# Output stores moved from SyncE's list to ScalarE's, in an attention and spatial-gate kernel

## The chip, the cores and the metric

The kernel runs on one core of a Trainium2 chip. A core has five engines with a list of instructions each: TensorE (PE, with its weight loads shown as PEld), VectorE (DVE), ScalarE (ACT), GpSimd (POOL) and SyncE (SP). An engine takes its list in order; engines wait for one another by semaphores. Transfers between HBM and the core's SBUF go over 16 DMA engines; an instruction on an engine's list issues them, and they run on their own afterwards. The metric is the device time of one execution in microseconds (us).

## The reference

For each of 8 batches and 8 heads, 576 tokens with 64 values each are first pooled into 32 memory slots, then attend to the slots; the result of all heads (512 values a token) goes through a gated feed-forward block whose gate mixes the tokens.

```python
a = softmax(phi, axis=slots)                      # 8 x 8 x 576 x 32
k_m, v_m = a^T k, a^T v                           # 32 x 64 per head
attn = softmax(q k_m^T / 8) v_m
x = attn, heads side by side                      # 8 x 576 x 512
h = relu(x @ w_in); u, v = halves of h            # 1024 -> 512 + 512
v_n = (v - mean) / sqrt(var + 1e-6)
v_s = w_spatial @ v_n + b_spatial                 # mixes the 576 tokens
out = (u * v_s) @ w_out                           # 8 x 576 x 512, float32
```

## The kernel before

The work goes batch by batch. A batch's 576 tokens are four tiles of 128 and a remainder of 64. Large products are made of three products of rounded parts (`fp32r`, a high and a low part of each factor), which is why most of PE's lines come in threes.

The stages are Python generators, each cut into steps by `yield`: `memory_weights` (loads phi, its exponentials), `memories` (loads k and v; product `kvm` over the tokens, line 342, and the scaled copies `kmn`, line 369, on ACT), `queries` (loads q in four pieces, transposes), `scores`, `products` (slots times `w_in`), `gate` (v's half: product `pv`, lines 621 and 630/631, its copies `vr`, lines 626 and 640 to 642, the normalization, and `vh`, line 663), `units` (u's half: product `pu`, line 687, read by ACT into `u`, line 696), `spatial` (the mixing, `ps`, line 725, and the gated product) and `project` (product `po`, line 765, and the output).

`project` is the stage at the change. It makes twelve matmuls into one PSUM bank `po` for a tile of 128 tokens; ACT copies the bank to an SBUF tile `o` (line 771); in the step after that, SP issues the store (line 774). The remainders of two batches share one tile: in every odd batch a fifth `po` is made, and it is stored by two issues, one for each batch (lines 776 and 777). So a batch has four or five copies, and the kernel has 36 copies and 40 stores.

What sets the order is written out by hand: three strings, `START`, `PLAN` (one pass for each of the batches 1 to 6) and `LAST`, list the steps; a letter names the stage (`O` for `project`), a digit the tile, a mark how many batches ahead. Each engine's list follows the order of the steps. While one batch is projected, the next one's gate and memory weights are on the way. A step of a store stands some steps behind the one of its copy.

Buffers: `o` has two, from the pool `two`, so a copy waits until the store two copies ago has landed. PSUM has four single banks (pool `ps1`: `po`, `pv`, `kvm` and others in turn) and two double ones (pool `ps2`: `pu`, `ps`), so PE's third `pu` needs the buffer that ACT empties by reading the first into `u`. A transfer counts on one of eight semaphores in turn, and an issue waits until the transfer before it on the same semaphore has landed, if that is not known from earlier waits.

All loads and stores are on SP's list. In a batch of the loop it holds: two stores, the phi load, two q loads, a store, the k load, the remaining stores, the v load, two more q loads.

Of the kernel before, what the change touches and what calls it, by code (L numbers as in the profile page):

```python
# [55 lines left out]
def memory_attention_spatial_gate(  # L56
# [29 lines left out]
    nc = tc.nc  # L86
    B, H, S, D = q.shape
# [3 lines left out]
    P = 128  # L91
    NI = 4
    SM = NI * P
    SR = S - SM
# [13 lines left out]
    def bank(name):  # L108
        return ps1.tile([P, 512], F32, tag="b1", name=name)
# [642 lines left out]
    def project(b, st):  # L752

        if st == NI and b % 2 == 0:
            return
        po = bank(f"po_{b}_{st}")
        n = 0
        for dt in range(NJ):
            if st < NI:
                h_, l_ = (x[:, dt, st * P : (st + 1) * P] for x in state["g", b])  # L760
            else:
                h_, l_ = (x[:, dt, :] for x in state["rem"])
            woh, wol = (x[:, dt % 2] for x in state["wo", dt // 2])
            for a, w in ((h_, woh), (h_, wol), (l_, woh)):
                nc.tensor.matmul(po, a, w, start=(n == 0), stop=(n == 11))  # L765
                n += 1
            if dt == 1:
                yield
        yield
        o = two.tile([P, DM], F32, name="o")  # L770
        nc.scalar.copy(o, po)  # L771
        yield
        if st < NI:
            nc.sync.dma_start(out[b, st * P : (st + 1) * P], o)
        else:
            nc.sync.dma_start(out[b - 1, SM:S], o[0:SR])
            nc.sync.dma_start(out[b, SM:S], o[SR:P])
        yield


    def warm_up(b, _):
# [13 lines left out]
    BATCH = {  # L795
        "P": memory_weights, "K": memories, "Q": queries, "S": scores, "M": products,
        "V": gate, "U": units, "G": spatial, "O": project,
    }
    threads, done = {}, {}
# [66 lines left out]
```

## Time and profile before

| what | us |
|---|---|
| median of 3 runs | 416.6 (416.01 to 416.63) |
| the profiled execution | 417.52 |
| its span, first to last instruction | 415.7 |
| PE busy | 401.5 (97%) |
| PE weight loads busy | 339.3 (82%) |
| DVE busy | 283.8 (68%) |
| ACT busy | 230.0 (55%) |
| POOL busy | 46.5 (11%) |

The granted TensorE clock is 0.8 of full speed in the second to fourth of forty slices of the span and 0.9 or more in the others. The 16 DMA engines are busy 42% of the span, in bursts. A row of the timeline gives an instruction's start from the start of the span and its duration; what stands in brackets is how long its engine had been idle and which instruction ended that. Issues of DMAs are work of an engine's sequencer (`SPq`) and are not counted as busy time.

### The profile page before, as it was taken

How to read it: one execution, taken by the hardware profiler on the slowest of the kernel's cores; microseconds unless marked ns; L12 is line 12 of the kernel's file. 1: busy time of each engine (PE TensorE's matmuls, PEld its weight loads, DVE VectorE, ACT ScalarE, POOL GpSimd, SP SyncE). 2: the span in 40 equal slices, each digit the busy share in tenths (PEclk: the TensorE clock that was granted, in tenths of full speed). 3: DMA queues.
4: the chain of work that ended last, by engine and by line, in shares of the span. 5: the costliest groups of instructions: out<-in, count | busy, mean ns of one | idle time of the engine just before them, and what ended most of it. 6: DMA issues, size and time to landing. Idle time of an engine off the chain costs nothing.

```text
span 415.7 us, 9467 instructions
## 1 busy us (share of the span) xinstructions
PE 401.5 (97%) x3965; PEld 339.3 (82%) x3965; DVE 283.8 (68%) x540; ACT 230.0 (55%) x425; POOL 46.5 (11%) x131
## 2 busy tenths in 40 slices
PE   6789999999999999999999999999999999999996
PEld 3544788989798888978798888988798788989984
DVE  1477999986988468947888468947887368924430
ACT  2468889546644476337644476347734476348321
POOL 1000321003200210003200210003200210013000
PEclk9888999999999999999999999999999999999999
DMA  8899595035810891039500990049401510020003
GB/s 297 320 383 279 116 342 142 2 107 111 236 50 31 176 301 24 0 105 276 123 2 17 247 258 7 0 117 290 97 2 37 101 50 0 2 76 27 0 30 97
DMA packets 85790, 50.70 MB, mean 122 GB/s; under 512 B 66226, under 2 KB 70322, under 8 KB 85748
## 3 DMA queue, kind: packets, MB, share of 16 engines
q1 hardware_dynamic: 85748, 50.10, 42.0%
q8 instruction: 31, 0.51, 0.5%
q14 instruction: 11, 0.09, 0.1%
HBM read 40.65 MB, written 9.44 MB: 120 GB/s over the span
## 4 chain that ended last, share of the span: by engine, by line
PE 87%; DMA 4%; DVE 4%; ACT 3%; issue 1%; SPq 0%; ACTq 0%
PE ps L725 29%; PE po L765 22%; PE pu L687 12%; PE pv L621 10%; PE kvm L342 3%; PE mp L589 3%; PE sc L523 2%; DMA w_rem<-in_moe_w_spatial_dram 2%; DMA q_all<-in_q_dram 1%; PE idle L785 1%; PE pv L630 1%; PE pv L631 1%; DMA out_dram<-o 1%; PE tq L410 1%; PE wt L255 1%
## 5 line engine op out<-in xcount | busy, mean ns | idle before, releaser
L725 PE MATMUL ps<-wth,vh 128*128 128x288 f32 x256 | 57.1, 304 | 0.0
L725 PE MATMUL ps<-wth,vl 128*128 128x288 f32 x256 | 54.8, 296 | 0.0
L725 PE MATMUL ps<-wtl,vh 128*128 128x288 f32 x256 | 54.5, 294 | 0.0
L765 PE MATMUL po<-woh,gl 128*128 128x512 f32 x128 | 50.4, 394 | 0.0
L765 PE MATMUL po<-woh,gh 128*128 128x512 f32 x128 | 50.4, 394 | 0.0
L645 DVE BATCH_NORM_STATS2 st<-vr 128x6 f32<-128x512 f32 (+1 forms) x40 | 27.0, 675 | 34.1 <-ACT vr L626 33.3
L765 PE MATMUL po<-wol,gh 128*128 128x512 f32 x128 | 50.2, 392 | 0.0
L725 PEld LDWEIGHTS ps<-wth,vh 128*128 128x128 f32 x256 | 41.2, 190 | 8.7 <-ACT vh L663 5.0
L650 POOL TENSOR_SCALAR rs<-mv 128x1 f32<-128x1 f32 (+1 forms) x40 | 8.8, 221 | 330.4 <-DVE grl L749 153.4
L747 ACT CAST gh<-g 128x512 fp32r<-128x512 f32 x32 | 19.8, 621 | 46.4 <-DVE g L736 45.2
L771 ACT COPY o<-po 128x512 f32<-128x512 f32 x36 | 21.0, 584 | 37.3 <-PE po L765 20.0
L725 PEld LDWEIGHTS ps<-wth,vl 128*128 128x128 f32 x256 | 41.1, 188 | 0.0
L725 PEld LDWEIGHTS ps<-wtl,vh 128*128 128x128 f32 x256 | 41.1, 188 | 0.0
L736 DVE TENSOR_TENSOR g<-u,ps 128x576 f32<-128x576 f32 x32 | 23.4, 751 | 17.1 <-PE ps L725 17.1
L665 DVE TENSOR_TENSOR vl<-vr,vh 128x512 fp32r<-128x512 f32 x32 | 21.6, 681 | 18.0 <-ACT vh L663 17.8
L660 ACT ACTIVATE vr<-vr,sh,rs 128x512 f32<-128x512 f32 (+1 forms) x40 | 32.1, 816 | 3.0 <-POOL sh L655 3.0
L626 ACT ACTIVATE vr<-pv 128x512 f32<-128x512 f32 x32 | 19.2, 600 | 19.4 <-PE pv L621 13.1
L687 PE MATMUL pu<-ah,mh 128*128 128x288 f32 x128 | 28.7, 306 | 0.0
L765 PEld LDWEIGHTS po<-wol,gh 128*128 128x128 f32 x128 | 24.1, 188 | 5.2
L765 PEld LDWEIGHTS po<-woh,gl 128*128 128x128 f32 x128 | 24.1, 188 | 5.2
L765 PEld LDWEIGHTS po<-woh,gh 128*128 128x128 f32 x128 | 24.0, 188 | 5.2
L687 PE MATMUL pu<-al,mh 128*128 128x288 f32 x128 | 27.4, 296 | 0.0
(141 smaller groups left out, 861.3 us busy)
## 6 DMA issues: line engine op xcount, KB each, us to landing
kv_sb<-in_k_dram SPq DMA_DIRECT2D x8, 1152.0 KB, 7.0
kv_sb<-in_v_dram SPq DMA_DIRECT2D x8, 1152.0 KB, 7.7
out_dram<-o SPq DMA_DIRECT2D x32, 256.0 KB, 2.3
q_sb<-in_q_dram SPq DMA_DIRECT2D x28, 288.0 KB, 5.6
phi_sb<-in_phi_dram SPq DMA_DIRECT2D x8, 576.0 KB, 5.0
raw<-in_moe_w_in_dram SPq DMA_DIRECT2D x8, 512.0 KB, 10.3
raw<-in_moe_w_out_dram SPq DMA_DIRECT2D x4, 512.0 KB, 6.0
q_all<-in_q_dram SPq DMA_DIRECT2D x1, 1152.0 KB, 5.4
```

The source lines that it names most:

```text
L342: nc.tensor.matmul(kvm[r][32 * j : 32 * j + 32], phi_sb[halves[r], j, i, :], kv_sb[halves[r], j, :, i * D : (i + 1) * D], start=(i == 0), ...
L621: nc.tensor.matmul(pv, x[:, r, cs], m[:, r, DM:DFF], start=(n == 0), stop=(n == 5))
L626: nc.scalar.activation(vr, pv, AF.Relu)
L645: nc.vector.bn_stats(st6, vr)
L660: nc.scalar.activation(vr, vr, AF.Identity, bias=sh, scale=rs)
L665: nc.vector.tensor_tensor(vl[:, st, :], vr, vh[:, st, :].bitcast(F32), op=ALU.subtract)
L687: nc.tensor.matmul(pu[:, hf, 0:HALF], m[:, r, cs], a[:, r, hf * HALF : (hf + 1) * HALF], start=(n == 0), stop=(n == 5),)
L725: nc.tensor.matmul(ps[:, hf, 0:HALF], a, w[:, hf * HALF : (hf + 1) * HALF], start=(n == 0), stop=(n == len(ops) - 1),)
L736: nc.vector.tensor_tensor(g.rearrange("p (a s) -> p a s", a=2), u[:, dt, :].rearrange("p (a s) -> p a s", a=2), ps[:, :, 0:HALF], op=ALU.mult,
L747: nc.scalar.copy(hi, x)
L765: nc.tensor.matmul(po, a, w, start=(n == 0), stop=(n == 11))
L771: nc.scalar.copy(o, po)
```

## The change

The three calls that issue the stores are made on ScalarE's queue.

```diff
         nc.scalar.copy(o, po)
         yield
         if st < NI:
-            nc.sync.dma_start(out[b, st * P : (st + 1) * P], o)
+            nc.scalar.dma_start(out[b, st * P : (st + 1) * P], o)
         else:
-            nc.sync.dma_start(out[b - 1, SM:S], o[0:SR])
-            nc.sync.dma_start(out[b, SM:S], o[SR:P])
+            nc.scalar.dma_start(out[b - 1, SM:S], o[0:SR])
+            nc.scalar.dma_start(out[b, SM:S], o[SR:P])
         yield
```

The first place is ACT's list in batch 1, around the third copy (`po_1_1` is the product of batch 1, tile 1; the number behind it is the buffer's):

```order
 L566 CAST ah<-aT 128x576
 L771 COPY o<-po_3_1645 128x512
+L774 DMA out_dram<-o 128x512 x2
 L771 COPY o<-po_1_1677 128x512
 L747 CAST grh<-g 128x64
 L626 ACTIVATE vr<-pv_1_1798 128x512
 L626 ACTIVATE vr<-pv_0_1809 128x512
+L774 DMA out_dram<-o 128x512
 L640 COPY vr<-pv_4_1838 64x512
 L642 ACTIVATE vr<-vr 64x512
```

Two issues now stand between the second copy and the third, and one between the copies of line 626 and that of line 640.

The second place is ACT's list a little later in the same batch, behind the copy of its last tile (the copy of the remainder stands just ahead of these rows):

```order
 L660 ACTIVATE vr<-vr,sh,rs 128x512
 L771 COPY o<-po_2_1866 128x512
+L776 DMA out_dram<-o 64x512
+L777 DMA out_dram<-o 64x512
 L369 ACTIVATE kmn<-kvm_0_1699,den 128x128
+L774 DMA out_dram<-o 128x512
 L663 CAST vh<-vr 128x512
 L369 ACTIVATE kmn<-kvm_1_1700,den 128x128
```

The remainder's two issues come ahead of the first `kmn`, the last tile's ahead of `vh`. An even batch has the last tile's alone.

The third place is SP's list for the same batch:

```order
 L330 DMA kv_sb<-in_k_dram 128x4x576
 L330 DMA kv_sb<-in_v_dram 128x4x576
-L774 DMA out_dram<-o 128x512 x2
 L297 DMA phi_sb<-in_phi_dram 128x4x288
 L427 DMA q_sb<-in_q_dram 32x72x32 x2
-L774 DMA out_dram<-o 128x512
 L330 DMA kv_sb<-in_k_dram 128x4x576
-L776 DMA out_dram<-o 64x512
-L777 DMA out_dram<-o 64x512
-L774 DMA out_dram<-o 128x512
 L330 DMA kv_sb<-in_v_dram 128x4x576
 L427 DMA q_sb<-in_q_dram 32x72x32 x2
```

The loads are left, in the order in which they stood. The instructions of PE, DVE and POOL keep their order, and so do ACT's others.

## Rows read from the trace of the kernel before

**Rows 1.** Page, busy time: us, share of the span, instructions
```profile
PE 401.5 (97%) x3965; PEld 339.3 (82%) x3965; DVE 283.8 (68%) x540; ACT 230.0 (55%) x425; POOL 46.5 (11%) x131
```

**Rows 2.** Page, the chain that ended last: shares by engine
```profile
PE 87%; DMA 4%; DVE 4%; ACT 3%; issue 1%; SPq 0%; ACTq 0%
```

**Rows 3.** Waits: who waited for whom, us in total, times, longest
```profile
ACT o L771 <- DMA out_dram<-o: 10.7, 4, 3.8
...
PEld pv L621 <- ACT o L771: 1.8, 2, 1.1
...
PE pv L621 <- ACT o L771: 1.0, 2, 0.7
```

**Rows 4.** Waits of SP's list, same columns
```profile
SPq L774 <- ACT o L771: 225.0, 14, 31.2
```

**Rows 5.** Instructions on out_dram: ns shortest/median/longest, starts; and landing
```profile
L774 SPq DMA_DIRECT2D out_dram<-o x32: 332/362/2613, 85.8 to 412.7; - x32
L776 SPq DMA_DIRECT2D out_dram<-o x4: 472/472/510, 144.2 to 409.9; - x4
L777 SPq DMA_DIRECT2D out_dram<-o x4: 588/592/609, 144.7 to 410.4; - x4
...
DMA to landing us min/median/max: 2.0/2.3/6.2
```

**Rows 6.** The chain in batch 5, 319 to 326 us: start, us, what
```profile
320.11 3.68 DMA out_dram<-o
...
323.89 0.59 ACT o L771
...
324.53 1.66 PE pv L621 x6
```

**Rows 7.** Timeline of ACT in batch 2: start, us, instruction, count [idle before, releaser]
```profile
185.46 0.59 ACT L771 COPY o<-po 128x512 f32<-128x512 f32 x1 [4.15 <-PE pv L621]
...
189.52 0.58 ACT L640 COPY vr<-pv 64x512 f32<-64x512 f32 x1 [1.12 <-PE pv L631]
```

**Rows 8.** Timeline of ACT in batch 4
```profile
282.29 0.58 ACT L640 COPY vr<-pv 64x512 f32<-64x512 f32 x1 [1.11 <-PE pv L631]
...
285.06 0.59 ACT L771 COPY o<-po 128x512 f32<-128x512 f32 x1
...
285.81 0.62 ACT L663 CAST vh<-vr 128x512 fp32r<-128x512 f32 x1
```

**Rows 9.** Timeline of ACT in batch 3
```profile
240.03 0.59 ACT L771 COPY o<-po 128x512 f32<-128x512 f32 x1 [1.45 <-PE po L765]
240.51 0.37 ACT L369 ACTIVATE kmn<-kvm,den 128x128 f32<-128x128 f32 x1
240.77 0.62 ACT L663 CAST vh<-vr 128x512 fp32r<-128x512 f32 x1
...
241.54 0.66 ACT L696 ACTIVATE u<-pu 128x576 f32<-128x576 f32 x1
```

**Rows 10.** Timeline of PE's weight loads in batch 3, the third pu
```profile
242.64 0.32 PEld L687 LDWEIGHTS pu<-ah,mh 128*128 128x128 f32 x2
```

**Rows 11.** Timeline of SP: issue of the third store in batches 1, 2, 4
```profile
141.82 1.43 SPq L774 DMA_DIRECT2D out_dram<-o  x1
...
187.86 2.61 SPq L774 DMA_DIRECT2D out_dram<-o  x1
...
281.22 1.32 SPq L774 DMA_DIRECT2D out_dram<-o  x1
```

**Rows 12.** Timeline of DVE and of PE's weight loads in batch 1
```profile
141.41 0.68 DVE L641 TENSOR_TENSOR vr<-vr,pv 64x512 f32<-64x512 f32 x1 [1.51 <-ACT vr L640]
...
143.12 0.19 PEld L765 LDWEIGHTS po<-woh,gh 128*128 128x128 f32 x1
```

**Rows 13.** Page, DMA queues: packets, MB, share of 16 engines' span
```profile
q8 instruction: 31, 0.51, 0.5%
```

## The prediction

> **What bounds the kernel now.** I read the busy times first. PE works 401.5 of 415.7 us and ACT 230.0 [rows 1], so PE sets the end and ACT has room on average. The chain of waits says the same: 87% of it is PE, 3% ACT, 4% DMA, and SP's queue 0% [rows 2]. A store can therefore matter in two ways only: PE waits for something that hangs on a store, or ACT, which empties PE's banks, comes late.
>
> Next the waits that have to do with stores. PE waited twice for a copy of L771, 1.8 us in all by its weight loads and 1.0 by its matmuls; the copy itself waited four times for a store's landing, 10.7 us [rows 3]. The reader should see how little that is: the change can win back at most these two waits of PE. SP's 225 us of waiting for the copy [rows 4] looks large, but it is SP that waits there. It stands ready when a copy ends, and what it holds back are loads, for which PE waits in no batch of the loop.
>
> The two waits of PE are in batches 5 and 2. In batch 5 the store took 3.68 us to land, against a median of 2.3 [rows 5, 6]; the third copy, which fills the same buffer, ended at 324.48, and PE went on at 324.53. In batch 2 the third copy began at 185.46 and ended at 186.05 after 4.15 us of idle time on ACT [rows 7]. In both the store was issued at once and was slow on the way: SP did not hold it.
>
> **The change part by part.** The 40 issues leave SP and stand in ACT's order, behind the step of the copy that frees them. I call a batch's copies A, B, C, E (the remainder, odd batches alone) and D, in ACT's order.
>
> *Stores A and B.* ACT issues them right behind copy B, whose end SP waited for as well. What follows on ACT is copy C, which has to wait for the landing anyway (the 10.7 us). Cost 0, gain 0: the slow landings were not SP's doing, so I leave them in.
>
> *Store C.* It stands between the two copies of L626 and L640. ACT is idle there for 1.11 us in batch 4, waiting for PE [rows 8]; an issue takes 0.36 (median of 32, [rows 5]). Cost 0, if the issue takes what it mostly took on SP. If that cover is gone, see the second rival.
>
> *Store D in batches 2 and 4.* Copy D runs from 285.06 to 285.65, and the cast of vh begins at 285.81 [rows 8]. The issue needs the end of copy D, so it lasts until 286.01, and vh begins 0.20 late. Everything up to the read of u is back to back and inherits this. The spare there: in batch 3 the read of u ends at 241.54 + 0.66 = 242.20, and the weight load of PE that needs its bank starts at 242.64 [rows 9, 10]. A load that waits starts 0.05 after ACT's end (324.48 to 324.53, [rows 6]), so 0.39 us are free; batches 2 and 4 have the same order of work. Cost 0, or 0.1 each if the issue also waits for the kmn ahead of it.
>
> *Stores E and D in batches 1, 3 and 5.* This is the term that I count. PE releases copy D at 240.03 [rows 9]. Right behind it in ACT's order come now the two halves of E (0.47 and 0.59 us on SP, [rows 5], with 0.04 between them), then the first kmn, then store D, then vh. Copy E is long done, so its issues start when copy D has been handed over, at about 240.06, and end at 241.16. The first kmn, which began at 240.51, begins then: 0.65 late. Store D's 0.36 runs beside kmn's 0.37, and vh begins at 241.58 instead of 240.77: 0.81 late. The read of u ends at 242.20 + 0.81 = 243.01, and PE's load starts at 243.06 instead of 242.64: 0.42 us, which PE, with no idle time here, does not get back. Three batches: 1.26 us.
>
> The trace has no DMA issue on ACT, so this needs bounds. From above: the issues might start only when copy D has ended (240.62). Then E ends at 241.72, kmn at 242.09, D at 242.45, vh is 1.68 late and PE 1.29 in each of three batches, with 0.1 twice more: 4.1. From below: an issue that holds up nothing behind it, 0. I take the value between, because kmn begins at 240.51, before copy D ends at 240.62 [rows 9]: ACT's sequencer hands an instruction over while the one ahead still runs, so it can issue beside a running copy; but nothing shows that work can pass an issue that stands ahead of it.
>
> The Trainium skill, page "Advanced Engine Details and Errata", section "Sequencer and Instruction Queues", says that further engine instructions can be read and queued while the sequencer's own code executes. By that the work behind E would be in ACT's queue already, and the sum would be the lower bound's 0. The overlap of kmn with copy D agrees with a queue; no row shows what is read during an issue. That is the first rival.
>
> *Batches 0, 6 and 7.* In batch 0 ACT has a long wait for PE behind the stores; in batch 7 each copy waits for twelve matmuls. In batch 6 one store D stands straight behind its copy, 0.36 plus the last of the copy. I take 0 and keep 0.5 as the bound. The last store starts behind the last copy as before: 0.
>
> *SP.* Loads no longer stand behind stores, so k and v go out earlier by the wait for copies E and D. Nobody waited for them: 0.
>
> Sum: 417.52 + 1.26 = 418.8 us for a profiled execution (its span of 415.7 and 1.8 around it). That execution is 0.9 over the median of the runs shown, so the median becomes 416.6 + 1.3 = **417.9 us**.
>
> **The rivals.**
>
> *First: the issues are hidden.* ACT works off a queue while its sequencer issues. For it speaks the overlap above; against it that an issue took 0.33 to 0.59 us of SP's sequencer, and that ACT's instructions too are handed over one by one. Time 416.6.
>
> *Second: store C is held up by SP's loads.* On SP the issue of store C took 1.43, 2.61 and 1.32 us in batches 1, 2 and 4 [rows 11], each behind two q loads; elsewhere it took 0.36. If what was full there is common to both engines, ACT is held until about the same moments, 143.25, 190.47 and 282.54. L640 began at 189.52 and 282.29 in batches 2 and 4 [rows 7, 8]; in batch 1, with its 0.58 us and L641 right behind it at 141.41 [rows 12], at 140.8. So it comes 2.45, 0.95 and 0.25 late. In batch 1 L641 ends at 142.09 and PE's load for the bank that it frees starts at 143.12 [rows 12]: 1.0 spare, 1.4 lost. In batch 3 the lateness lies between and fits into this. In batches 2 and 4 it adds to store D's 0.20 and meets the 0.39: 0.8 and 0.1. With 1.3 for E and D: 416.6 + 1.3 + 2.3 = 420.2. Against it: SP's own list, in which one issue waits for the one before, explains the long ones without anything common.
>
> The Trainium skill, page "DMA: Bandwidth & Descriptors", section "Queues, rings and completion order", says that SP and ACT own a row of rings each, but no descriptor generator of their own. That speaks for this rival and its 420.2; the trace, with every transfer of the kernel on one queue, can't show it.
>
> *Third, and on the other side: the slow landings go.* Place: copy C in batches 5 and 2; price: the two waits of PE, between 1.0 and 1.8 us [rows 3], say 1.4. It decides when the landing falls below about 3 us. For it: in batch 5 two q loads came right behind the stores on the same queue, and in the new order they stand right behind the pair ahead of them, long before. Against it: in batch 2 no load was that near, and the stores were slow all the same. What both may share is one of the 31 fetches of instructions, 16 KB each [rows 13], which stay, since PE's program does. With the issues hidden: 415.2; with them at 1.3: 416.5.
>
> *Fourth: issue and copy don't overlap,* the upper bound: 416.6 + 4.1 = 420.7.
>
> **How the numbers follow.** Forecast 0.42, first rival 0.20, second 0.15, third 0.16 (0.12 of it with the issues hidden), fourth 0.07. About 0.2% (0.8 us) is what a measurement of this kernel can tell from no change. Of the forecast I put 0.10 within that, as the 0.42 us of a batch may be 0.25. Faster: 0.12. Same: 0.10 + 0.20 + 0.04 = 0.34. Slower: 0.32 + 0.15 + 0.07 = 0.54. The range of 415.6 to 420.4 leaves out the third rival's best and the fourth; the forecast's own is 417.2 to 418.6.
>
> **What would show it.** In the new trace, in batches 1, 3 and 5, the first kmn should begin 1.1 us after copy D instead of 0.48, and PE's weight load of the third pu should wait for the read of u, by some 0.4 us; in batches 2 and 4 it should not. Store C's issue on ACT should take 0.36; 1.3 or more means the second rival. PE's two waits for copy C should still be there, behind landings near 4 us. If kmn follows copy D as before, the first rival is right and the time does not change; if both landings are near 2.3, the third.

## The result, and the profile after

The changed kernel took 420.51 us (median of 6 runs, 418.81 to 421.29), the kernel before 416.62 (median of 6). The ratio is 1.0076, with a 95% interval of 1.0052 to 1.0100: slower by 3.2 us (2.2 to 4.2). The forecast was 417.9, slower by 1.3. So the direction and the place were right and the size was too small; the median lies 0.1 us above the end of the range, the ratio's 419.8 inside it. Two more comparisons of the same two kernels, on other chips, gave 1.0056 (1.0017 to 1.0095) and 1.0070 (1.0031 to 1.0108).

The page's busy times and its chain by engine, which answer to [rows 1, 2]:

```profile
PE 401.2 (96%) x3965; PEld 338.0 (81%) x3965; DVE 284.2 (68%) x540; ACT 231.2 (55%) x425; POOL 49.0 (12%) x131
...
PE 80%; ACT 6%; DVE 5%; DMA 5%; issue 2%; ACTq 1%; POOL 1%; SPq 0%
```

PE works as long as before, and the chain now leaves PE for ACT more often. The waits of the changed kernel show what is behind that (us in total, times, longest), to be read against [rows 3]:

```profile
ACT o L771 <- DMA out_dram<-o: 14.3, 5, 3.7
...
PEld pu L687 <- ACT u L696: 1.9, 3, 0.7
...
PE pu L687 <- ACT u L696: 1.3, 3, 0.4
...
PEld pv L621 <- ACT o L771: 1.1, 2, 0.6
...
PE pv L621 <- ACT o L771: 0.2, 1, 0.2
```

The waits for u are new, three in number and in batches 1, 3 and 5. The waits for copy C are still there. ACT's timeline in batch 3, the stretch of [rows 9] (ACTq is the issue on ACT's sequencer):

```profile
240.15 0.59 ACT L771 COPY o<-po 128x512 f32<-128x512 f32 x1 [1.45 <-PE po L765]
240.16 0.50 ACTq L776 DMA_DIRECT2D out_dram<-o  x1
240.69 0.61 ACTq L777 DMA_DIRECT2D out_dram<-o  x1
241.35 0.37 ACT L369 ACTIVATE kmn<-kvm,den 128x128 f32<-128x128 f32 x1 [0.61 <-ACT o L771]
241.43 0.52 ACTq L774 DMA_DIRECT2D out_dram<-o  x1
241.99 0.62 ACT L663 CAST vh<-vr 128x512 fp32r<-128x512 f32 x1 [0.27 <-issue]
242.52 0.36 ACT L369 ACTIVATE kmn<-kvm,den 128x128 f32<-128x128 f32 x1
242.78 0.64 ACT L696 ACTIVATE u<-pu 128x576 f32<-128x576 f32 x1
```

E's two issues begin 0.01 us after copy D was handed over and run beside it. The first kmn begins 0.05 us after the second issue has ended (240.69 + 0.61 = 241.30), 1.20 us behind copy D instead of 0.48. PE's weight loads of the third pu in the three odd batches, the stretch of [rows 10]:

```profile
149.67 0.30 PEld L687 LDWEIGHTS pu<-ah,mh 128*128 128x128 f32 x2 [0.67 <-ACT u L696]
...
243.47 0.30 PEld L687 LDWEIGHTS pu<-ah,mh 128*128 128x128 f32 x2 [0.65 <-ACT u L696]
...
337.41 0.30 PEld L687 LDWEIGHTS pu<-ah,mh 128*128 128x128 f32 x2 [0.63 <-ACT u L696]
```

In batch 3 the read of u ended at 242.78 + 0.64 = 243.42, and the load stood ready at 243.47 - 0.65 = 242.82. The sum of the three waits is 1.95 us, where a loss of 1.26 was forecast.

The issues on ACT (ns shortest, median, longest) and the landing of store L774, against [rows 5]:

```profile
L774 ACTq DMA_DIRECT2D out_dram<-o x32: 333/338/647, 86.2 to 414.0; - x32
...
DMA to landing us min/median/max: 2.0/3.1/6.5
```

An issue takes mostly what it took on SP, but the one of store D right behind E took 0.52. A landing is no faster: by the same view of L774 the median was 2.3 us in all three traces of the kernel before, and 3.0 to 3.1 in the three of the changed one.

### The profile page after: what moved, and what is told of

The parts are those of the page before. It is cut to its first block, busy times and chain, and to the rows that moved or that the text cites. A ratio compares the mean times of both kernels' runs of the same rounds, so it can differ in the third digit from the quotient of the medians.

```text
span 417.0 us, 9465 instructions
## 1 busy us (share of the span) xinstructions
PE 401.2 (96%) x3965; PEld 338.0 (81%) x3965; DVE 284.2 (68%) x540; ACT 231.2 (55%) x425; POOL 49.0 (12%) x131
## 4 chain that ended last, share of the span: by engine, by line
PE 80%; ACT 6%; DVE 5%; DMA 5%; issue 2%; ACTq 1%; POOL 1%; SPq 0%
PE ps L725 28%; PE po L765 20%; PE pu L687 10%; PE pv L621 8%; PE mp L589 3%; PE kvm L342 3%; DMA w_sb<-in_moe_w_spatial_dram 2%; PE sc L523 2%; DMA out_dram<-o 2%; DMA q_all<-in_q_dram 1%; ACT o L771 1%; PE wt L255 1%; DVE phi_sb L316 1%; PE idle L785 1%; PE pv L631 1%
## 5 line engine op out<-in xcount | busy, mean ns | idle before, releaser
L771 ACT COPY o<-po 128x512 f32<-128x512 f32 x36 | 21.0, 584 | 36.4 <-PE po L765 21.7
```

## The experiments

Of every kernel I take the ratio to the kernel before on the same chip and, from its trace, the time from the start of batch 1's products kvm (at 91.97 us in the first trace of before, 91.61 in that of the changed kernel) to the end of the span. This stretch leaves out the first 90 us, which differ from one execution to the next. Its waits are those of PE's weight loads. The span is printed to 0.1 us, so a stretch is good to 0.05.

| kernel | ratio (95% interval) | stretch, us | waits for u | waits for copy C |
|---|---|---|---|---|
| before, three traces | 1.0011 (0.9981 to 1.0041) | 323.73, 323.84, 323.75 | 0 | 1.8, 2.1, 1.8 |
| after, three traces | 1.0076, 1.0056, 1.0070 | 325.39, 326.17, 326.30 | 1.9, 2.0, 1.9 | 1.1, 2.1, 2.1 |
| E on SP | 0.9999 (0.9963 to 1.0035) | 323.84 | 0 | 1.3 |
| only E on ACT | 1.0030 (1.0002 to 1.0058) | 325.84 | 1.7 | 2.1 |
| only batch 0 on ACT | 0.9989 (0.9961 to 1.0016) | 324.58 | 0 | 2.6 |
| E behind its copy | 1.0009 (0.9988 to 1.0029) | 324.80 | 0 | 2.5 |
| three buffers for o, stores on SP | 0.9955 (0.9931 to 0.9979) | 322.61 | 0 | 0 |
| three buffers for o, E behind its copy | 0.9945 (0.9918 to 0.9972) | 322.25 | 0 | 0 |
| E in four issues (4 runs) | 1.0180 (1.0144 to 1.0215) | 331.74 | 6.5 | 2.3 |
| D in two issues, E behind its copy | 1.0066 (1.0032 to 1.0100) | 325.27 | 2.3 | 0.9 |

Taking the last two columns from the stretch leaves 321.7 to 322.9 us in every row, where the stretches themselves lie between 322.3 and 331.7: past the start, these two waits are most of what sets the kernels apart. The 1.2 us that are left were not traced further.

### The changed kernel again

No edit.

> The changed kernel itself, once more. Its six times lie 2.2 to 4.2 us above the kernel before, while its one profiled execution accounts for less: between the starts of the products kvm of batches 1 and 6 and the end it lost 1.66 us (1.95 of it PE's waits for the read of u in batches 1, 3 and 5), and 0.7 us near 63 to 69 us, where GpSimd's sh took 2.03 us while two q loads ran that went out at 91.7 us before. Theory 1, the loss is the stores' issues on ACT: the three waits of 0.63 to 0.67 us stand there again, and nothing else new recurs; ratio 1.004 to 1.008. Theory 2, a good part is the earlier q loads at 62 us: sh at 63 us takes over 1.5 us again and PE's wait behind it of 0.7 us recurs. Theory 3, chance (the stretches at 1.2 GHz in the first 50 us, and where slow store landings fall): the waits in other places differ between the two profiles, and the ratio's interval reaches below 1.005.

Measured: 419.78 against 418.22, ratio 1.0056. The three waits for u were there again (0.68, 0.64 and 0.63 us). So was the long sh, 3.86 us this time, but it stood also in the kernels below that don't have the q loads early: theory 2 was not borne out. Chance plays in as well: copy C's waits were 2.1 us instead of 1.1.

### Store E on SP again

```diff
-            nc.scalar.dma_start(out[b - 1, SM:S], o[0:SR])
-            nc.scalar.dma_start(out[b, SM:S], o[SR:P])
+            nc.sync.dma_start(out[b - 1, SM:S], o[0:SR])
+            nc.sync.dma_start(out[b, SM:S], o[SR:P])
```

> The changed kernel with the remainder's two issues (store E) on SP again, stores A to D on ACT. Theory 1 (the issues of E ahead of kmn, vh and u cost PE its three waits of 0.63 to 0.67 us): PE's waits for u go, and the kernel is 1.9 us faster than the changed one, so 417 to 418.5. Theory 2 (the q loads that no store holds back any more): nothing of that changes here, the kernel stays 2 us or more above the one before. If store D's own issue is the one that matters, u's wait stays at some 0.1 to 0.4 us in all five batches.

Measured: 418.01, ratio 0.9999, no wait for u. Stores A, B, C and D on ACT cost nothing that shows (the interval reaches 1.5 us to either side); the loss goes with E. Theory 2 fell here: the q loads were early as in the changed kernel, and no loss shows.

### Only store E on ACT

```diff
         else:
-            nc.sync.dma_start(out[b - 1, SM:S], o[0:SR])
-            nc.sync.dma_start(out[b, SM:S], o[SR:P])
+            nc.scalar.dma_start(out[b - 1, SM:S], o[0:SR])
+            nc.scalar.dma_start(out[b, SM:S], o[SR:P])
```

> The kernel before with only store E's two issues on ACT, A to D on SP. Theory 1: kmn begins 1.1 us behind copy D in batches 1, 3 and 5 and PE waits for u there; without D's 0.5 us issue behind kmn the wait is 0.1 to 0.4 us instead of 0.65, so 0.3 to 1.2 us in all, 417 to 418. Theory 2: the q loads are back behind SP's stores, so no loss at 69 us, and the kernel is within 1 us of the one before. If it costs 3 us, E is all of the change's loss.

Measured: 419.19, ratio 1.0030, waits for u of 1.7 us, more than the 0.3 to 1.2 expected. ACT's timeline in batch 3 has the largest part of the difference:

```profile
240.15 0.47 ACTq L776 DMA_DIRECT2D out_dram<-o  x1
240.65 1.15 ACTq L777 DMA_DIRECT2D out_dram<-o  x1
241.85 0.37 ACT L369 ACTIVATE kmn<-kvm,den 128x128 f32<-128x128 f32 x1 [1.18 <-issue]
```

The second issue took 1.15 us, and PE waited 0.82. In batch 5 it took 0.61, kmn began 0.76 us later than in [rows 9], and the wait was the smallest of the three, 0.3 (1.7 less 0.82 and 0.58). That is what E alone does without store D, as expected. In this trace E and its long issues make most of the loss; how often an issue is long, one trace does not show.

### Only batch 0's stores on ACT

```diff
-            nc.sync.dma_start(out[b, st * P : (st + 1) * P], o)
+            (nc.scalar if b == 0 else nc.sync).dma_start(out[b, st * P : (st + 1) * P], o)
```

> The kernel before with only batch 0's four stores issued by ACT, all others by SP. SP then issues batch 2's second pair of q loads at about 62 us instead of 91.7, as in the changed kernel, and the loop is as before. Theory 1: within 0.5 us of the kernel before. Theory 2: sh takes some 2 us at 63 us, PE waits 0.7 us behind it, and the kernel is 0.7 to 2 us slower than the one before.

Measured: 417.16, ratio 0.9989. The earlier q loads of the start cost nothing that shows.

### E's issues directly behind E's own copy

```diff
         nc.scalar.copy(o, po)
-        yield
+        if st < NI:
+            yield
         if st < NI:
```

> The changed kernel with store E's two issues directly behind E's own copy instead of some steps later, all stores still on ACT. In the changed kernel's trace ACT idles 1.45 us between vr (line 660) and copy D, so 1.15 us of issues fit in there. Theory 1 (E's place ahead of kmn is what costs): kmn starts 0.48 us behind copy D again, PE's three waits of 0.63 to 0.68 us for u go, and the kernel is 1.5 to 2 us faster than the changed one, within 0.5 us of the kernel before. Rival (that ACT issues stores at all, or E's landing later in the batch, is what costs): still 1.5 us or more above the kernel before.

Measured: 418.52 against 417.58, ratio 1.0009. ACT's timeline in batch 1 (the lines of the issues are one or more higher, as the edit adds a line):

```profile
143.02 0.59 ACT L771 COPY o<-po 128x512 f32<-128x512 f32 x1 [0.78 <-PE po L765]
143.64 0.54 ACTq L777 DMA_DIRECT2D out_dram<-o  x1
144.21 0.61 ACTq L778 DMA_DIRECT2D out_dram<-o  x1
144.87 0.81 ACT L660 ACTIVATE vr<-vr,sh,rs 128x512 f32<-128x512 f32 x1 [1.26 <-POOL sh L655]
145.77 0.59 ACT L771 COPY o<-po 128x512 f32<-128x512 f32 x1
146.26 0.37 ACT L369 ACTIVATE kmn<-kvm,den 128x128 f32<-128x128 f32 x1
146.39 0.35 ACTq L775 DMA_DIRECT2D out_dram<-o  x1
```

The idle time ahead of vr is put down to POOL, but vr begins 0.05 us after the issue has ended: it is the issue. It fills the 1.45 us that ACT had free ahead of copy D. kmn is 0.49 us behind copy D, and PE waits for u nowhere. All 40 stores are on ACT, and the steady loss is gone: it was E's place.

### E in four issues instead of two

```diff
-            nc.scalar.dma_start(out[b - 1, SM:S], o[0:SR])
-            nc.scalar.dma_start(out[b, SM:S], o[SR:P])
+            for h in (slice(0, 256), slice(256, DM)):
+                nc.scalar.dma_start(out[b - 1, SM:S, h], o[0:SR, h])
+                nc.scalar.dma_start(out[b, SM:S, h], o[SR:P, h])
```

> The changed kernel with each of store E's two issues split into two of half the columns: four issues instead of two at the same place, the same bytes. Theory 1 (time on ACT's list): some 1.1 us more of issues ahead of kmn, so PE's waits for u in batches 1, 3 and 5 grow from 0.65 to about 1.7 us, and the kernel is 3 us slower than the changed one (423 to 424). Rival (the stores' traffic or their landing is what costs): no more than 0.5 us slower than the changed one.

Measured: 426.01, ratio 1.0180, 4.6 us over the third comparison of the changed kernel (1.0180 - 1.0070, of 416 us). PE's weight loads of the third pu in batches 1 and 3:

```profile
152.98 0.30 PEld L687 LDWEIGHTS pu<-ah,mh 128*128 128x128 f32 x2 [1.97 <-ACT u L696]
...
249.50 0.30 PEld L687 LDWEIGHTS pu<-ah,mh 128*128 128x128 f32 x2 [2.62 <-ACT u L696]
```

The waits grew by 6.5 - 1.95 = 4.55 us, which is that loss. It is more than the 3 us expected, as four issues took 2.5 us and the last of batch 3 alone 1.30. The bytes are the same, so their number by itself is not the cause.

### Store D in two issues, E behind its copy

```diff
         if st < NI:
-            nc.scalar.dma_start(out[b, st * P : (st + 1) * P], o)
+            parts = (slice(0, 256), slice(256, DM)) if st == 2 else (slice(0, DM),)
+            for h in parts:
+                nc.scalar.dma_start(out[b, st * P : (st + 1) * P, h], o[:, h])
```

> From the kernel with E's issues directly behind E's copy (1.0009 of before): store D's one issue, which stands between kmn and vh in every batch, is split into two of half the columns. It tests the spare time that the prediction gave store D: 0.39 us, of which one issue uses some 0.2. Theory 1: a second issue of 0.34 to 0.6 us makes vh and the read of u later by as much, 0.2 of it is still hidden, and PE waits 0.2 to 0.4 us for u in each of batches 1 to 5, so 1 to 2 us over the unsplit kernel, 1.003 to 1.006 of before. Rival (u has far more spare time, E's cost came from its traffic): no waits of PE for u, and within 0.3 us of the unsplit kernel.

Measured: 419.33, ratio 1.0066, against 1.0009 without the split. ACT's timeline in batch 1:

```profile
145.44 0.59 ACT L771 COPY o<-po 128x512 f32<-128x512 f32 x1
145.92 0.37 ACT L369 ACTIVATE kmn<-kvm,den 128x128 f32<-128x128 f32 x1
146.06 0.85 ACTq L777 DMA_DIRECT2D out_dram<-o  x2
146.95 0.62 ACT L663 CAST vh<-vr 128x512 fp32r<-128x512 f32 x1 [0.66 <-issue]
...
147.74 0.64 ACT L696 ACTIVATE u<-pu 128x576 f32<-128x576 f32 x1
```

PE's third pu waited 0.32 us for it, 0.33, 0.35 and 0.49 in batches 2 to 4, and 0.29 and 0.52 in batches 5 and 6: 2.3 us in all, a little more than the 1 to 2 expected. One issue of store D is free and two are not: the spare time is there, and it is small.

### Three buffers for o

The stores stay on SP:

```diff
-        o = two.tile([P, DM], F32, name="o")
+        o = three.tile([P, DM], F32, name="o")
```

> The kernel before, stores on SP, with three buffers for o instead of two: copy C then waits for the landing of the store three copies ago. If the landing of store A is what PE waits for ahead of the products pv in batches 2 and 5 (1.08 and 0.74 us in the trace of before, up to 1.3 in others), these waits go and the kernel is 1 to 2.5 us faster. If the wait only moves to the next thing (po's bank, the copies of line 626), it stays within 0.5 us.

Measured: 415.86 against 417.58, ratio 0.9955. What copy L771 still waits for, with the stretch's waits for copy C gone:

```profile
ACT o L771 <- PE po L765: 21.4, 14, 2.2
...
ACT o L771 <- ACT o L771: 0.8, 1, 0.8
```

No copy waits for a landing, and PE waits for no copy ahead of pv.

### Three buffers and E behind its copy, all stores on ACT

From the changed kernel:

```diff
-        o = two.tile([P, DM], F32, name="o")
+        o = three.tile([P, DM], F32, name="o")
         nc.scalar.copy(o, po)
-        yield
+        if st < NI:
+            yield
         if st < NI:
```

> All stores on ACT, E's issues directly behind E's copy, three buffers for o. If the two costs are separate, this is as the kernel before with three buffers for o, 1 to 2.5 us faster than the kernel before, and nothing is gained by ACT over SP. If SP's late loads or SP's issue lag cost something, it is another 0.5 us or more faster than that one.

Measured: 415.58, ratio 0.9945. It beats both kernels, as the version on SP does; the two intervals overlap nearly whole, so which engine issues decides nothing once E's place and the buffer are mended.

### The kernel before against itself, and the changed one a third time

No edits.

> The kernel before, unchanged, against itself: ratio 1.000, with an interval that shows what this comparison can tell. Its trace is a second one of before. If the longer sh at 63 us (2.03 us or 3.86 us in all the traces but the first of before, where it took 0.77) belongs to the change, it takes 0.77 us here again; if it is chance, it takes 2.03 or 3.86 here too.

> The changed kernel a third time, on the same chip as the kernel before against itself. Theory 1: three waits of PE for u of 0.63 to 0.68 us, 1.9 to 2.0 in all, which is the whole of the steady loss: ratio 1.004 to 1.006, and waits for copy C between 1.0 and 2.2 us as in before. If the first result (1.0076) holds a second steady loss, the ratio is again over 1.007.

> The kernel before, a third look, for GpSimd's sh near 63 us alone. In both traces of before it took 0.77 us, in the ten traces of other kernels 2.03 or 3.86, also where the change's stores are not in it. If the two short ones are the program's own, it takes 0.77 again, and then 0.5 us of PE's wait behind it counts against the change as it stands; if they are chance, it takes 2.03 or 3.86 here.

Measured: before 1.0011 (0.9981 to 1.0041), after 1.0070 (1.0031 to 1.0108) on the same chip. The second trace of before had sh at 0.77 us, the third at 2.03, with PE's wait of 0.71 behind it: the long sh comes without the change as well. It stood in one of three traces of before and in all eleven traces of other kernels, so whether it comes more often in those is not shown.

## Why the prediction came out as it did

**Stores E and D in the odd batches: the right step, mis-sized.** The forecast had PE's load start 0.42 us late. In batch 3 it started 243.47 - 240.15 = 3.32 us behind copy D, where the kernel before had 242.64 - 240.03 = 2.61 [rows 9, 10]: 0.71 late. The bounds of 0 and 1.29 held. Two parts of the term were off. E's issues to kmn: 0.72 us late instead of 0.65 (0.50 + 0.61 with gaps of 0.03 and 0.05 around, for 0.47 and 0.59). Store D: it was taken to run wholly beside kmn for 0.36 us, but it began 0.08 behind kmn's start and took 0.52, so vh was 1.10 late instead of 0.81. The read of u then began 242.78 - 240.15 = 2.63 us behind copy D instead of 1.51: 1.12 late. The spare time was right: 1.12 - 0.71 = 0.41, the forecast's 0.39 and the 0.02 by which the read itself took less (0.64 us for 0.66). The same account holds elsewhere. In batch 1 of the kernel with four issues u was 152.29 - 148.34 - 1.51 = 2.44 late and the load 152.98 - 148.34 - 2.61 = 2.03; with store D in two, u was 0.79 late and the load 0.38. The load is late by the lateness of u less 0.41.

The wait of 0.65 is a little less than 0.71, as it counts from the end of the load ahead, and of loads that wait for nothing one runs 0.06 us past the start of the next. What PE lost in the end, its next products sc (line 523) show, in batch 3 of the kernel before and of the changed one:

```profile
247.74 0.47 PE L523 MATMUL sc<-qT,kT 64*32 64x288 f32 x8
...
248.53 0.47 PE L523 MATMUL sc<-qT,kT 64*32 64x288 f32 x8
```

They began 7.71 us behind copy D before and 8.38 after, 0.67 late; in batches 1 and 5 it is 0.70 and 0.65, so 2.0 us in all for the 1.26.

**The rest of the loss.** In the stretch of the table the changed kernel lost 2.2 us on average (325.95 against 323.77), of which 2.0 are these. The three comparisons gave 3.2, 2.3 and 2.9 us. Their intervals hold 2.2, the first just so (2.2 to 4.2). Whether another half to one us is lost in the first 90 us stays open: batch 1's kvm began between 89.6 and 95.8 us in these traces, and no experiment shows a steady part of that. PE's wait of 0.71 us behind GpSimd's long sh can be part of it (see the kernel before against itself). Runs of one kernel differ by their mean granted clock as well: in the third comparison the changed kernel took 417.68 us in the run with the highest, 0.999, and 423.72 in the one with the lowest, 0.980.

**First rival, issues hidden: wrong.** Nothing that stood behind an issue on ACT began before it had ended: kmn 0.05 us after E's, vr 0.05 us after E's in the other place. By the Trainium skill, page "Advanced Engine Details and Errata", section "Sequencer and Instruction Queues", this work could have been queued during the issue, and the loss would have been 0; in no trace here did it pass the issue. The Trainium skill, page "Perfetto Trace Analysis", section "DMA Instruction — HWDGE (DVE, Sync)", has the sequencer free for its next instruction only when the issue has ended; the 0.05 us agree with that.

**Second rival, store C held up by SP's loads: wrong.** Store C's issue on ACT in batches 1 and 2:

```profile
139.18 0.34 ACTq L774 DMA_DIRECT2D out_dram<-o  x1
...
187.97 0.40 ACTq L774 DMA_DIRECT2D out_dram<-o  x1
```

and what SP issues there, in batch 1:

```profile
135.83 4.71 SPq L427 DMA_DIRECT2D q_sb<-in_q_dram  x1
140.65 1.77 SPq L330 DMA_DIRECT2D kv_sb<-in_k_dram  x1
```

ACT's issue passed while SP's q load was at it. The long time behind the q loads [rows 11] stayed with SP and now falls on the k load.

**Third rival, the slow landings go: wrong.** The chain of the changed kernel in batch 2, the like of [rows 6]:

```profile
182.07 3.43 DMA out_dram<-o
...
185.58 0.59 ACT o L771
...
186.22 1.65 PE pv L621 x6
```

The landing that copy C waits for took 3.43 us, in batch 5 3.59, and PE's two waits are still there. Over all traces with two buffers they lie between 0.3 and 1.4 us each, and of what was tried only the third buffer removes them.

The prediction called these stores issued at once. That holds from the end of copy B; copy A, whose store copy C waits for, had ended before. In batch 5 of the kernel before:

```profile
317.68 0.57 ACT L771 COPY o<-po 128x512 f32<-128x512 f32 x1
...
320.11 0.84 SPq L774 DMA_DIRECT2D out_dram<-o  x2
```

Store A was issued 1.86 us behind the end of its copy, at 318.25, and the changed kernel keeps that order. An issue right behind copy A was not tried.

**Fourth rival: wrong.** Issue and copy do overlap (240.16 against 240.15).

**The steps at 0** held: stores A, B and C, store D in batches 2 and 4, and SP's earlier loads, by the kernel with E on SP. In batches 2 and 4 of the changed kernel u was 0.28 us late where 0.20 was forecast, within the spare 0.41.

## What to carry to other kernels

Here the issue of a store took 0.3 to 0.6 us of ACT's list in most cases, and whatever stood behind it came that much later. Put an issue where its engine waits anyway, and behind the instructions that the bounding engine needs. To price such a move, find the first instruction behind the issue for which the bounding engine waits, and its spare time; what goes beyond the spare counted in full here, once for each of the three odd batches. When a store's landing is what holds a copy, look for another buffer: here it removed the wait, and another engine to issue did not.

## What the runs showed of the hardware that was not expected

Twice an issue on ACT took about double its usual time: E's last took 1.15 us with E alone on ACT and 1.30 us with E in four issues, both in batch 3, instead of 0.61. The second of them:

```profile
246.05 1.30 ACTq L778 DMA_DIRECT2D out_dram<-o  x1
```

In the first case SP issued a store and a 1152 KB load beside it, in the second SP issued nothing; in both, the DMA engines were at such loads, and one fetch of instructions fell into the stretch. Loads alone do not do it: in batch 1 of the kernel with four issues the DMA engines were as busy, and the last issue took 0.61. What does it was not separated.

GpSimd's sh on 64 rows near 63 us took 0.77, 2.03 or 3.86 us, and ended 0.04 to 0.13 us after the end of a VectorE instruction each time: the first, the second or the fourth that began while it ran. In the third trace of before:

```profile
63.50 2.03 POOL L655 TENSOR_SCALAR sh<-mv,rs 64x1 f32<-64x1 f32 x1
```

and VectorE there:

```profile
63.54 0.68 DVE L665 TENSOR_TENSOR vl<-vr,vh 128x512 fp32r<-128x512 f32 x1
64.14 1.34 DVE L543 TENSOR_TENSOR sm<-sm,rmx 128x1152 f32<-128x1152 f32 x1
```

sh ended at 65.53, VectorE's second instruction at 65.48.

Where sh took 3.86 us, PE's weight loads waited 1.27 and 1.18 us behind it. In the second trace of the changed kernel the granted clock fell after these waits (the stretches 60 to 75 and 75 to 95 us; behind the five busy times stand the clock, the DMA share and GB/s):

```profile
60.00:75.00 15.00, 13.01 (x106) 10.99 (x105) 11.54 (x16) 11.52 (x18) 4.63 (x3) 0.93 0.78 164
75.00:95.00 20.00, 20.00 (x111) 17.92 (x111) 18.52 (x33) 9.85 (x18) 0.00 (x0) 0.97 0.07 27
```

In finer stretches it was 1.00 up to 72 us, 0.64 from 72 to 75, 0.87 from 75 to 80 and 1.00 again behind that, so it lay at the lower level, 1.2 GHz, for some 3.5 us (an estimate from these shares). With E on SP the same two waits left the clock at 1.00 in both stretches. From the end of the second wait (71.12 us there, 71.78 here) to batch 1's kvm it took 22.54 us there against 24.05.
